# A long convolution with a gate: the first transform split by even and odd rows, in plain float32, with regrouped inputs

## The chip, the cores and the metric

The kernel runs on one core of a Trainium2 chip. The metric is the device time of one execution in microseconds (us). Matrix products run on TensorE (PE; its weight loads are PEld), elementwise work on VectorE (DVE), ScalarE (ACT) and GpSimd (POOL); SyncE (SP) and ACT issue the DMA transfers. The granted clock is the share of full speed that TensorE's clock was given.

## The reference

Four sequences of 12800 positions and 128 channels are convolved with a filter that a small network makes from `pos_emb`, multiplied by x, and sent through a gated projection. Cut to what matters:

```
h = maximum(pos_emb @ w1, 0) @ w2 * exp(-0.01 * pos)      # the filter
u = x * v                                                 # (4, 12800, 128) float32
y = x * irfft(rfft(u, 2 S) * rfft(h, 2 S))[:S]            # long convolution, S = 12800
gate = sigmoid(sum over k of conv_w[k] * y shifted by k)  # five taps
out = (gate * (y @ w_val)) @ w_out
```

Everything is float32, except that the weights of the gate arrive as 64-bit floats and are narrowed in the kernel.

## The kernel before

A position is written as s = 6400 j + 64 n1 + n2 with J = 2 blocks j, N1 = 100 and N2 = 64, and the Fourier transform of 6400 points is done in two steps, over n1 (a matrix of 100 by 100) and over n2 (one matrix of 64 by 64, complex, for each k1). The program has three phases.

The **first phase** (lines 179 to 307) does the step over n1. The signal part, `signal()` (lines 263 to 291), goes through 64 chunks, one for each j and each pair of n2 (P1C = 2). `fetch` (243 to 249) brings x and v of a chunk into one tile `ld`, 100 partitions (n1), in rows of 1 KB (two n2 by 128 channels); `_Split` (93 to 101) issues each transfer as one of 96 partitions and one of 4, on SP. `prep` (251 to 259) makes the product on DVE (`u_t`), a rounded copy on ACT (`u_hi`, of a type that TensorE reads in fewer steps than plain float32) and the remainder on POOL (`u_lo`). For two batches b at a time and for the cosine and the sine table (c), three matmuls of 512 columns are summed in one PSUM tile `fp`: hi x hi, table remainder x hi, hi x remainder (line 281). ACT empties the cosine tiles into `st` (284), DVE the sine tiles (286). Two stores per chunk then write `st` to `a_u` in DRAM (288 to 291), the cosine part from ACT's queue, the sine part from SP's.

Between the chunks runs the filter part, `filt()` (lines 184 to 237), in three sections: `pos_emb` is loaded with n1 in the partitions, transposed by TensorE (`tp`, 194), copied by DVE (`posT`, 198), multiplied by w1 (`gp`, 202) and cut and windowed by DVE into `g_sb` (206); then `ap` is the filter's step over n1, in plain float32 with two matmuls for the two halves of the output partitions (220, 221), copied by ACT to `ag` (222); last, for each k1, a scaled table `fk` is made by ACT and DVE (231, 232), multiplied (`gp`, 234) and copied back by ACT (236). The loop at lines 296 to 303 deals out the filter's steps among the 128 steps of the signal by a table of costs (297); a scheduler then sets the order on each engine by its own timing. PSUM has eight banks: four for `fp`, one for `tp`, one for `gp`, two for `ap`.

The **second phase** (313 to 430) reads `a_u` back for two k1 at a time, does the step over n2, multiplies by the filter's spectrum and goes back, in an order written out by hand, and writes `c_y`. The **third phase** (440 to 610) undoes the step over n1, transposes, and applies the gate.

## Time and profile before

| what | value |
|---|---|
| median of 3 runs | 1340.4 us (1333.96 to 1342.48) |
| the profiled execution | 1342.08 us, its span 1340.2 us |
| mean granted clock | 0.938 |
| PE / DVE / ACT / POOL busy | 88% / 80% / 47% / 52% of the span |
| moved by DMA | 332.90 MB, 248 GB/s over the span |
| first phase, to its last evacuation | 401 us, 109.55 MB moved |

The profile is of one execution. In its lists of groups a row is one line of the program on one engine: line, engine, operation, tile written <- tiles read, shapes, count | busy time in us, mean ns of one | idle time of the engine just before them and what ended it. A plain float32 matmul appears as two records, so a count of 128 there is 64 matmuls. In views by stretch of time a row gives the stretch, its length, then for each engine its busy time and, in brackets, the number of records, then the granted clock, the mean busy share of the 16 DMA engines and GB/s. In the order of time a row is start, length, engine, line, operation; where several records are merged, the length is that of all. In the DMA view, q1 holds what SP issues and q10 what ACT issues: packets, MB, share of the 16 engines' time in the stretch.

### The profile page before, as it was taken

Reading aid. Unit: us, or ns where it says so; the run is one execution under the profiler, and the core shown is the slowest. Engines: PE = TensorE matmul, PEld = TensorE weight load, DVE = VectorE, ACT = ScalarE, POOL = GpSimd, SP = SyncE. Lnnn points to the kernel's source line nnn. Section 1 sums busy time; section 2 is a strip of 40 time slices with the busy share of each in tenths; the row PEclk is TensorE's granted clock in tenths of the full one; section 3 lists DMA queues with packets and bytes.
Section 4 is the critical chain, followed back from the end, with each engine's and each line's share of the span. In section 5 each row is a group of like instructions: output and inputs, shape, how many; then the busy total and the mean of one; then the engine's idle time right before and its main releaser. Section 6 shows DMA issues by size and latency. Waiting matters only on the chain. (4 is left out here: it accounts for less than half of the span.)

```text
span 1340.2 us, 16163 instructions
## 1 busy us (share of the span) xinstructions
PE 1184.8 (88%) x5464; PEld 554.0 (41%) x5464; DVE 1068.8 (80%) x1130; ACT 635.5 (47%) x1064; POOL 693.8 (52%) x346
## 2 busy tenths in 40 slices
PE   4879999788686899999999999578999898999986
PEld 3657877566452333333333333122333333333332
DVE  5875343988456999999999999127999999999997
ACT  3334545677442333333333333134665666666663
POOL 2333234444454799999999999234333333333230
PEclk8888899889888999999999999656999999999999
DMA  9999788889987677778787874766989898889842
GB/s 250 285 312 297 232 253 271 245 268 306 296 261 285 219 278 280 281 277 279 280 280 279 280 266 173 209 160 157 254 236 246 234 243 243 244 247 243 241 145 98
DMA packets 144571, 332.90 MB, mean 248 GB/s; under 512 B 11166, under 2 KB 63434, under 8 KB 136554
## 3 DMA queue, kind: packets, MB, share of 16 engines
q1 hardware_dynamic: 96576, 226.13, 57.9%
q10 hardware_dynamic: 47914, 105.76, 21.7%
q8 instruction: 43, 0.70, 0.2%
q14 instruction: 38, 0.31, 0.1%
HBM read 200.77 MB, written 131.07 MB: 248 GB/s over the span
## 5 line engine op out<-in xcount | busy, mean ns | idle before, releaser
L534 DVE SCALAR_TENSOR_TENSOR gt<-ext,cw,gt 128x1600 f32<-128x1600 f32 x128 | 298.3, 2330 | 0.0
L258 POOL TENSOR_TENSOR u_lo<-u_t,u_hi 100x1024 fp32r<-100x1024 f32 x64 | 158.7, 2483 | 239.0 <-ACT u_hi L257 199.9
L519 POOL TENSOR_TENSOR ext<-yr,ld 128x400 f32<-128x400 f32 x120 | 134.1, 1117 | 280.4 <-DVE yr L517 275.1
L375 ACT COPY c_sb<-c_ps 128x1024 f32<-128x1024 f32 x100 | 101.3, 1013 | 275.3 <-PE c_ps L368 275.3
L340 PE MATMUL z_ps<-ld 128*64 128x512 f32 x800 | 194.4, 605 | 7.8 <-DMA ld<-a_u 6.6
L427 POOL TENSOR_TENSOR va<-va,vb 128x1024 f32<-128x1024 f32 x50 | 158.0, 3160 | 37.1 <-DVE vb L345 37.0
L281 PE MATMUL fp<-u_hi,fwd_hi 100*100 100x512 f32 x256 | 117.8, 460 | 55.2 <-ACT st L284 26.4
L492 PE MATMUL sd<-ld,inv 100*64 100x512 f32 x512 | 155.6, 681 | 9.8 <-issue 7.7
L286 DVE COPY st<-fp 100x512 f32<-100x512 f32 x128 | 85.4, 685 | 71.8 <-PE fp L281 52.9
L345 DVE TENSOR_TENSOR vb<-z_ps,h_sb 128x2048 f32<-128x2048 f32 x50 | 114.5, 2291 | 24.9 <-ACT c_sb L375 24.7
L506 PE MATMUL tp<-ident,sd_sb 128*128 128x128 f32 x512 | 90.7, 304 | 45.7 <-ACT sd_sb L499 45.7
L499 ACT COPY sd_sb<-sd 128x512 f32<-128x512 f32 x128 | 74.6, 583 | 115.5 <-PE sd L492 115.4
L553 PE MATMUL o_ps<-gd,wout 128*128 128x400 f32 x256 | 119.4, 548 | 8.4 <-DVE gd L548 8.2
L428 POOL TENSOR_TENSOR vc<-vc,vd 128x1024 f32<-128x1024 f32 x50 | 118.5, 2370 | 15.2 <-DVE vd L345 10.3
L256 DVE TENSOR_TENSOR u_t<-ld 100x1024 f32<-100x1024 f32 x64 | 86.9, 1359 | 48.4 <-POOL u_lo L258 33.6
L345 DVE TENSOR_TENSOR va<-z_ps,h_sb 128x2048 f32<-128x2048 f32 x50 | 114.0, 2281 | 11.0 <-DMA ld<-a_u 11.0
L429 POOL TENSOR_TENSOR va<-va,vb 128x1024 f32<-128x1024 f32 x50 | 118.6, 2371 | 0.0
L506 PEld LDWEIGHTS tp<-ident,sd_sb 128*128 128x128 f32 x512 | 58.6, 151 | 132.9 <-ACT sd_sb L499 132.9
L281 PE MATMUL fp<-u_hi,fwd_lo 100*100 100x512 f32 x256 | 110.0, 430 | 0.0
L368 PE MATMUL c_ps<-vc,ld 64*128 64x512 f32 x400 | 100.6, 621 | 10.7 <-DVE vc L418 10.6
L543 PE MATMUL v_ps<-ext,wval 128*128 128x400 f32 x256 | 108.5, 506 | 0.0
L257 ACT CAST u_hi<-u_t 100x1024 fp32r<-100x1024 f32 x64 | 68.0, 1064 | 77.4 <-PE fp L281 37.0
(76 smaller groups left out, 1895.6 us busy)
## 6 DMA issues: line engine op xcount, KB each, us to landing
c_y<-c_sb ACTq DMA_DIRECT2D x100, 512.0 KB
ld<-a_u SPq DMA_DIRECT2D x49, 1024.0 KB
ld<-c_y SPq DMA_DIRECT2D x64, 768.0 KB
ld<-in_xt_dram SPq DMA_DIRECT2D x32, 800.0 KB
out_dram<-o_sb ACTq DMA_DIRECT2D x32, 800.0 KB
ld<-in_x_dram SPq DMA_DIRECT2D x64, 384.0 KB
ld<-in_v_dram SPq DMA_DIRECT2D x64, 384.0 KB
a_u<-st ACTq DMA_DIRECT2D x64, 384.0 KB
```

The source lines that it names most:

```text
L258: nc.gpsimd.tensor_tensor(lo, u_t, hi.bitcast(F32), op=ALU.subtract)
L281: nc.tensor.matmul(out=fp, lhsT=w[:, c], rhs=d[:, b:b + 2], start=(k == 0), stop=(k == 2))
L340: nc.tensor.matmul(out=z[half[h]], lhsT=wk[:, h, half[c]], rhs=a2[:, h, j], start=True, stop=True)
L345: nc.vector.tensor_tensor(out, z.rearrange("p (b d) -> p b d", d=D).unsqueeze(1).to_broadcast([128, n, B, D]), h_sb.unsqueeze(2).to_broadc ...
L427: nc.gpsimd.tensor_tensor(va[:, 0:2], va[:, 0:2], vb[:, 0:2], op=ALU.add)
L428: nc.gpsimd.tensor_tensor(vc, vc, vd, op=ALU.add)
L429: nc.gpsimd.tensor_tensor(va[:, 2:4], va[:, 2:4], vb[:, 2:4], op=ALU.add)
L492: nc.tensor.matmul(out=sd[c * N2:(c + 1) * N2], lhsT=inv[:, c], rhs=ct[c][:, r * B * D:(r + 1) * B * D], start=True, stop=True)
L506: nc.tensor.transpose(out=tp[:, b], in_=t[:, b], identity=ident)
L519: nc.gpsimd.tensor_tensor(e[:, r0 + r], yr, xr, op=ALU.mult)
L534: nc.vector.scalar_tensor_tensor(gt, rows(t, k), cw[:, k:k + 1], gt, op0=ALU.mult, op1=ALU.add)
L553: nc.tensor.matmul(out=o_ps, lhsT=wout, rhs=gd, start=True, stop=True)
```

## The change

It has three parts, all in the first phase.

*Even and odd n1.* With n1 = 2 a + h, the transform's matrix at k1 + 50 equals that at k1 for even n1 and is its negative for odd n1. The 50 even rows are put into partitions 0 to 49 and the 50 odd ones into partitions 64 to 113, each with a table of 50 by 100 (50 k1, cosine and sine; `fwd2`). For each n2 of a chunk there are then two matmuls, `ev` and `od`, in two different row tiles of the array, 512 columns (4 batches by 128 channels), in plain float32, without the split into a rounded part and a remainder. ACT copies `od` to SBUF (`od_sb`); DVE writes `ev` + `od_sb` (k1 from 0 to 49) and `ev` - `od_sb` (k1 from 50 to 99) into `st`. The product is made on POOL for the even rows and on DVE for the odd ones, both on 50 partitions of 1024 columns. The PSUM banks are two each for `ev`, `od`, `gp` and `ap`. The stores of a chunk now hold the sums (ACT's queue) and the differences (SP's queue).

*x and v* are arranged by the host as one array `xv` in which a chunk's row of one partition (x and v, two n2, four batches) is contiguous, 8 KB; they are loaded three chunks ahead instead of two, the two halves of the partitions in separate transfers, each split into 48 and 2 partitions.

*Positions* are arranged as `post`, with (n2, feature) already in the partitions: the transposes `tp` and copies `posT` go, and one transfer of 128 partitions replaces four.

The core of the diff:

```diff
@@ -97,7 +102,8 @@
     def dma_start(self, out, in_):
-        for a, b in ((0, 96), (96, N1)):
+        n = out.shape[0]
+        for a, b in ((0, n // 16 * 16), (n // 16 * 16, n)):
             self.eng.dma_start(out=out[a:b], in_=in_[a:b])
...
+                pos_sb = load()[:, 0:J * HC // 2 * N1].rearrange("p (j q a) -> p j q a", j=J, q=HC // 2)
+                nc.sync.dma_start(out=pos_sb, in_=post[:, c0 // HC])
                 for j in range(J):
                     for n in range(0, HC, 8):
-                        tp = ps1.tile([128, 4, N1], F32, name="tp", bufs=1)
-                        for q in range(4):
-                            nc.tensor.transpose(
...
-                        nc.vector.tensor_copy(out=posT, in_=tp)
-                        yield
-                        gp = ps1.tile([N1, 8, FO], F32, name="gp", bufs=1)
+                        gp = ps1.tile([N1, 8, FO], F32, name="gp", bufs=2)
...
-                                lhsT=posT[:, q], rhs=w1bd, start=True, stop=True)
+                                lhsT=pos_sb[:, j, n // 2 + q], rhs=w1bd, start=True, stop=True)
...
+        H1 = N1 // 2
+        par = [slice(h * 64, h * 64 + H1) for h in range(2)]
...
             j, n0 = chunks[i]
...
+            t = load()
+            for h in range(2):
+                sync_s.dma_start(out=t[par[h]], in_=xv[j, h, n0 // P1C])
+            return t.rearrange("a (w e) -> a w e", w=2)
 
         def prep(i):
...
-            nc.vector.tensor_tensor(u_t, x_t, v_t, op=ALU.mult)
-            nc.scalar.copy(out=hi, in_=u_t)
-            nc.gpsimd.tensor_tensor(lo, u_t, hi.bitcast(F32), op=ALU.subtract)
-            return hi, lo
...
+            u_t = p1.tile([128, P1C, B * D], F32, name="u_t", bufs=3)
+            for h, eng in enumerate((nc.gpsimd, nc.vector)):
+                eng.tensor_tensor(
+                    u_t[par[h]].rearrange("a n e -> a (n e)"), t[par[h], 0], t[par[h], 1], op=ALU.mult)
+            return u_t
+
+        ahead = [fetch(0), fetch(1), fetch(2)]
...
-                for b in range(0, B, 2):
-                    for c in range(2):
-                        fp = ps1.tile([N1, 2, P1C, D], F32, name="fp", bufs=4)
-                        for k, (w, d) in enumerate(((fwd_hi, hi), (fwd_lo, hi), (fwd_hi, lo))):
-                            nc.tensor.matmul(out=fp, lhsT=w[:, c], rhs=d[:, b:b + 2], start=(k == 0), stop=(k == 2))
-                        o = st[:, c, :, b:b + 2].rearrange("k n b d -> k b n d")
-                        if c == 0:
-                            nc.scalar.copy(out=o, in_=fp)
-                        else:
-                            nc.vector.tensor_copy(out=o, in_=fp)
+                u_t = ready.pop(0)
+                st = p1.tile([N1, 2, P1C, B * D], F32, name="st", bufs=3)
+                for n in range(P1C):
+                    ev = ps1.tile([N1, B * D], F32, name="ev", bufs=2)
+                    od = ps1.tile([N1, B * D], F32, name="od", bufs=2)
+                    for h, o in enumerate((ev, od)):
+                        nc.tensor.matmul(out=o, lhsT=fwd2[par[h]], rhs=u_t[par[h], n], start=True, stop=True)
+                    od_sb = p1.tile([N1, B * D], F32, name="od_sb", bufs=2)
+                    nc.scalar.copy(out=od_sb, in_=od)
+                    nc.vector.tensor_tensor(st[:, 0, n], ev, od_sb, op=ALU.add)
+                    nc.vector.tensor_tensor(st[:, 1, n], ev, od_sb, op=ALU.subtract)
                     yield
-                for c in range(2):
-                    (scalar_s if c == 0 else sync_s).dma_start(
...
+                for s in range(2):
+                    (scalar_s if s == 0 else sync_s).dma_start(
+                        out=a_u[s * H1:(s + 1) * H1, :, ns, j].rearrange("k c n b d -> (k c) n (b d)"),
+                        in_=st[:, s])
```

The scheduler orders the new instructions anew. Two places matter below. The first is PE while the filter's `ap` matmuls run beside the signal's (the second section of `filt`). Before, the signal's matmuls come in runs between runs of the filter's:

```order
L220 MATMUL ap<-fwd,g_sb 64x100
L221 MATMUL ap<-fwd,g_sb 64x100
L281 MATMUL fp<-u_hi,fwd_hi 100x512
L281 MATMUL fp<-u_hi,fwd_lo 100x512
L281 MATMUL fp<-u_lo,fwd_hi 100x512
L281 MATMUL fp<-u_hi,fwd_hi 100x512
L281 MATMUL fp<-u_hi,fwd_lo 100x512
L281 MATMUL fp<-u_lo,fwd_hi 100x512
```

In the changed program (L208 and L209 are the filter's matmuls of before's L220 and L221, L267 is the signal's; `fwd_66` is the table `fwd2`):

```order
L208 MATMUL ap<-fwd,g_sb 64x100
L267 MATMUL ev<-u_t,fwd_66 100x512
L209 MATMUL ap<-fwd,g_sb 64x100
L267 MATMUL od<-u_t,fwd_66 100x512
L208 MATMUL ap<-fwd,g_sb 64x100
L209 MATMUL ap<-fwd,g_sb 64x100
```

The runs are cut up: an `ev` and its `od` are apart, with a filter matmul between them, and the shape changes from row tiles to column tiles and back around each.

The second place is DVE while the scalings `fk` run (the third section of `filt`). Before, two copies of `st` and one product stand between them for each chunk:

```order
L232 SCALAR_TENSOR_TENSOR fk<-dft,tw,fk 128x128
L286 COPY st<-fp 100x2x2x128 x2
L232 SCALAR_TENSOR_TENSOR fk<-dft,tw,fk 128x128 x4
L256 TENSOR_TENSOR u_t<-ld 100x1024
L232 SCALAR_TENSOR_TENSOR fk<-dft,tw,fk 128x128 x4
L286 COPY st<-fp 100x2x2x128 x2
```

In the changed program (L220 is now the scaling, L243 the product of the odd rows, L270 and L271 the sum and the difference):

```order
L243 TENSOR_TENSOR u_t<-ld 50x1024
L220 SCALAR_TENSOR_TENSOR fk<-dft,tw,fk 128x128 x4
L270 TENSOR_TENSOR st<-ev,od_sb 100x512
L271 TENSOR_TENSOR st<-ev,od_sb 100x512
L220 SCALAR_TENSOR_TENSOR fk<-dft,tw,fk 128x128 x4
L270 TENSOR_TENSOR st<-ev,od_sb 100x512
L271 TENSOR_TENSOR st<-ev,od_sb 100x512
L243 TENSOR_TENSOR u_t<-ld 50x1024
```

For each chunk four operations of 512 columns stand now where two stood; the scalings and the product keep their places.

63 lines of the change are left out of this document (21 added, 42 removed).

## The prediction

> **What bounds the kernel now.** I read the page first, then the busy time of the engines by stage, then the instructions of single lines by stage, and last the order of time inside the stage that matters.
>
> ```profile
> span 1340.2 us, 16163 instructions
> PE 1184.8 (88%) x5464; PEld 554.0 (41%) x5464; DVE 1068.8 (80%) x1130; ACT 635.5 (47%) x1064; POOL 693.8 (52%) x346
> ```
>
> These shares are means over three phases with different limits. The diff touches the first phase alone, so that phase has to be cut out. Its last store into `st` ends near 401 us. I cut it at the times at which 12, 36 and 52 of its 64 chunks were done:
>
> ```profile
> 0.00:94.00 94.00, 63.91 (x294) 46.56 (x295) 63.58 (x113) 30.21 (x46) 32.38 (x17) 0.87 0.96 281
> 94.00:253.00 159.00, 152.56 (x1137) 116.56 (x1136) 76.22 (x93) 82.38 (x121) 58.10 (x24) 0.95 0.88 263
> 253.00:346.00 93.00, 74.52 (x358) 55.36 (x356) 76.43 (x130) 66.72 (x149) 41.60 (x18) 0.91 0.90 279
> 346.00:401.00 55.00, 42.25 (x144) 26.45 (x144) 28.46 (x34) 23.02 (x36) 26.82 (x11) 0.84 0.87 280
> 401.00:1340.20 939.20, 851.60 (x3536) 309.04 (x3536) 824.09 (x764) 433.21 (x714) 534.89 (x278) 0.95 0.75 238
> ```
>
> The columns are length, PE, PEld, DVE, ACT and POOL busy, then granted clock, DMA share and GB/s. Stage 1 (0 to 94) belongs to the DMA engines: share 0.96, no engine over 64 of 94 us. Stage 2 (94 to 253) belongs to PE, busy 152.56 of 159. Stage 3 (253 to 346) belongs to nobody alone: DVE 76.43 and PE 74.52 of 93, DMA 0.90. Stage 4 is transfers again (0.87), with every engine below 43 of 55. How many chunks a stage holds is read from the evacuations on DVE, two per chunk, and what else DVE does in stage 3 from line 232:
>
> ```profile
> 0.00:94.00 94.00, 15.97 (x24) 0.87 0.96 281
> 94.00:253.00 159.00, 32.30 (x48) 0.95 0.88 263
> 253.00:346.00 93.00, 21.08 (x33) 0.91 0.90 279
> 346.00:401.00 55.00, 15.95 (x25) 0.84 0.87 280
> ...
> 253.00:346.00 93.00, 38.60 (x80) 0.91 0.90 279
> ```
>
> So stage 2 is where the filter's transform (L220, L221) runs between the signal's matmuls, and stage 3 is where 80 of the 100 `fk` scalings (38.60 us of DVE) run between the signal's evacuations. The 939 us behind 401 have the same instructions in both kernels and are taken as unchanged.
>
> **The change part by part.** Prices first.
>
> ```profile
> L281 PE MATMUL fp<-u_hi,fwd_hi 100*100 100x512 f32 x256 | 117.8, 460 | 55.2 <-ACT st L284 26.4 <-ACT u_hi L257 18.5 <-DVE st L286 9.6
> L256 DVE TENSOR_TENSOR u_t<-ld 100x1024 f32<-100x1024 f32 x64 | 86.9, 1359 | 48.4 <-POOL u_lo L258 33.6 <-DMA a_u<-st 9.5 <-DMA ld<-in_x_dram 3.1
> L286 DVE COPY st<-fp 100x512 f32<-100x512 f32 x128 | 85.4, 685 | 71.8 <-PE fp L281 52.9 <-DMA a_u<-st 18.8
> L232 DVE SCALAR_TENSOR_TENSOR fk<-dft,tw,fk 128x128 f32<-128x128 f32 x100 | 48.9, 538 | 10.3 <-ACT fk L231 10.3
> L234 PE MATMUL gp<-fk,ag 128*128 128x128 f32 x200 | 29.2, 291 | 4.4 <-ACT ag L236 3.2 <-DVE fk L232 1.2
> L202 PE MATMUL gp<-w1bd,posT 128*100 128x128 f32 x128 | 19.8, 305 | 2.8 <-DVE posT L198 2.8
> ...
> L548 DVE TENSOR_TENSOR gd<-v_ps,sg 128x400 f32<-128x400 f32 x128 | 71.6, 559 | 3.5 <-PE v_ps L543 2.3 <-ACT sg L538 1.1
> L516 DVE TENSOR_TENSOR yr<-tp,dif 128x204 f32<-128x204 f32 x128 | 46.0, 360 | 63.6 <-ACT dif L508 44.7 <-DMA ld<-c_y 18.7 <-ACT o_sb L561 0.2
> ```
>
> DVE. Two copies of 512 columns per chunk (L286) become four sums and differences of one PSUM and one SBUF operand. That form is at L548 (400 columns, 559 ns) and L516 (204 columns, 360 ns): 199 ns for 196 columns, so 512 columns take 559 + 114 = 673 ns, about what the copy takes. Net: two more per chunk, 1.35 us per chunk, 86 us over the phase. The product (L256) stays, since 50 partitions of 1024 columns take as long as 100; half of it goes to POOL, in the place of `u_lo`. The 16 copies of `posT` leave DVE. ACT loses the cast (L257) and keeps one evacuation of 512 columns per column n, into `od_sb` now. A wait is added there: ACT's store of a chunk waited for ACT's own copies and now waits for DVE's second sum, and the next `od_sb` copies, which DVE's next sums need, stand behind it.
>
> ```profile
> 181.58 0.72 ACTq L101 DMA_DIRECT2D a_u<-st  x2
> ...
> L284 ACT COPY st<-fp 100x512 f32<-100x512 f32 x128 | 70.9, 592 | 70.2 <-PE fp L281 46.4 <-DMA a_u<-st 15.6 <-DMA ld<-in_v_dram 5.6
> ```
>
> From there ACT needs 0.72 + 0.59 = 1.3 us, while DVE still has a difference and a product to do, 0.67 + 1.36 = 2.0 us: covered. Uncovered, 1.3 - 0.7 = 0.6 us a chunk would be 10 us in the 16 chunks of stage 3, within the upper end below.
>
> PE. Three matmuls of 512 columns for each of four PSUM tiles become one `ev` and one `od` in plain float32 for each of two columns n. In order of time, first the seam of stage 2, then a plain float32 row-tile pair of the second phase, and the weight loads beside the latter:
>
> ```profile
> 180.14 0.31 PE L221 MATMUL ap<-fwd,g_sb 100*64 100x100 f32 x1
> 180.38 0.47 PE L281 MATMUL fp<-u_hi,fwd_hi 100*100 100x512 f32 x1
> ...
> 182.50 0.31 PE L221 MATMUL ap<-fwd,g_sb 100*64 100x100 f32 x1
> ...
> 182.65 0.31 PE L221 MATMUL ap<-fwd,g_sb 100*64 100x100 f32 x1
> ...
> 184.13 0.39 PE L281 MATMUL fp<-u_hi,fwd_lo 100*100 100x512 f32 x1
> 184.36 0.40 PE L281 MATMUL fp<-u_lo,fwd_hi 100*100 100x512 f32 x1
> 184.69 0.39 PE L220 MATMUL ap<-fwd,g_sb 100*64 100x100 f32 x1
> ...
> 521.98 1.99 PE L368 MATMUL c_ps<-va,ld 64*128 64x512 f32 x8
> 523.90 1.08 PE L327 MATMUL z_ps<-w2bd,ag 128*64 128x256 f32 x8
> ...
> 522.52 0.19 PEld L368 LDWEIGHTS c_ps<-va,ld 64*128 64x128 f32 x2 [0.24 <-issue]
> 522.95 0.19 PEld L368 LDWEIGHTS c_ps<-va,ld 64*128 64x128 f32 x2 [0.24 <-issue]
> ```
>
> At full clock an old matmul takes 0.23 us (184.13 to 184.36). A plain float32 matmul has two records; in the second phase each takes a step of 0.43 us (522.52 to 522.95) whether one or both halves of the rows work in it, so a pair takes 0.86 us and a lone one also 0.86. Eight records, two pairs, take 1.92 us (521.98 to 523.90). A filter matmul pair takes two steps of 0.15 (182.50 to 182.65). A change of shape costs 0.10 more than the same step without it (184.36 to 184.69 is 0.33; 180.14 to 180.38 is 0.24).
>
> In the order of the changed program, the `ev` and `od` of stages 1 and 4 mostly stand side by side (18 and 23 pairs), and PE has room there. In stage 2 the scheduler puts filter matmuls between them. Counted from its rows for chunks 12 to 36: 4 pairs and 88 lone ones, 147 pairs and 55 lone filter matmuls, 178 changes of shape. Before, the same chunks have 288 old matmuls, 185 pairs and 14 lone filter matmuls, 78 changes of shape, and 56 small matmuls (transposes, L202, L234) against 11 now, 0.3 us each by L202 and L234. After: 92 x 0.86 + 202 x 0.29 + 178 x 0.10 + 3 = 159 us. Before: 288 x 0.233 + 199 x 0.29 + 78 x 0.10 + 17 = 150 us. Stage 2 took 159 us, 9 us more than its sum. Below, if PE never waits: 159, no change; above, if the small matmuls are priced at full clock (17 becomes 12) and the remainder stays: +13. I take **+10**.
>
> DVE in stage 3: 76.43 + 32 x 0.673 = 98 us, and 84 instead of 80 scalings, 2 more: 100 us in a stage of 93. Below, without any idle time: +7; above, with all of the 16.6 us in which DVE now idles there: +24. DVE will seldom wait in a stage that it limits, so about 3 us of idle: **+10**.
>
> Transfers. Bytes stay; x and v come in rows of 8 KB instead of 1 KB, in the same number of issues on SP (four loads of 48 and 2 partitions per chunk for four of 96 and 4), and with three chunks ahead instead of two. Queue q1 in stages 1 and 4, in the second phase (4 and 8 KB rows to 128 partitions) and in the third (8 KB rows to 96), and q10 (2 KB stores) in stage 2:
>
> ```profile
> q1 hardware_dynamic: 16895, 20.98, 76.4%
> ...
> q1 hardware_dynamic: 6945, 10.18, 57.7%
> ...
> q1 hardware_dynamic: 13351, 56.68, 41.6%
> ...
> q1 hardware_dynamic: 11868, 75.90, 63.1%
> ...
> q10 hardware_dynamic: 5060, 9.42, 19.4%
> ```
>
> The second column is MB, the third the share of 16 engines. Bytes per engine and ns: 18.3 now (20.98 MB in 0.764 x 94 us x 16), 21.3 in the second phase (0.416 x 400 us x 16), 15.7 in the third (0.631 x 480 us x 16). Stage 1 loads some 16 MB (20.98 less the stores), 55 us of all engines; at 21.3 it gains 8 us, at 15.7 it loses 9. Stage 4 loads 5 MB: 3 us either way. The new loads reach fewer partitions at once than either row; between ends that far apart I take **0** for both stages and keep the ends. DVE there needs 63.6 + 24 x 0.67 less 7 for `posT`, 73 of 94 us, and 45 of 55: hidden under the transfers.
>
> Sum: 0 + 10 + 10 + 0 = +20 on a span of 1340.2, so 1360. The profiled execution is within 2 us of the median of the runs, 1340.4, so the same 20 gives **1360 us**.
>
> [...]
>
> **The rivals.**
>
> *Lone row tiles overlap after all* (faster): PE starts `od` while `ev` still runs, with the filter's short matmuls slipped through. For it: pairs do overlap in the second phase. Against: every change of shape in the rows above costs time, and the filter's weights fill 100 rows, both tiles. Price: 88 lone matmuls become 44 pairs, 38 us less on PE; stage 2 then falls to its transfers, 0.88 of 159 or 140 us, some 20 us shorter, and with -8, +7 and -3 elsewhere: 1316.
>
> *Gains and losses cancel* (no change): loads run at 21.3 in stages 1 and 4 (-8, -3) and PE does not wait in stage 2 (0), since the chain product, cast, remainder is gone, while DVE still costs 10: 1339.
>
> *Loads to half of the partitions run at half the rate* (slower), 10.7: 4.8 us of loads per chunk and 2.7 us of stores (q10: 9.42 MB in 0.194 x 159 us x 16, 19.1), 7.5 us x 64 = 480 against 401: 1419. For it: the third phase's 15.7 on 96 partitions against 21.3 on 128. Against: loads and stores of different engines interleave.
>
> *DVE is shut out by POOL* (slower). The products read two SBUF operands on both engines at once now:
>
> ```profile
> L256 DVE TENSOR_TENSOR u_t<-ld x64: 1207/1217/3405, 7.1 to 392.3; 100x1024 f32<-100x1024 f32 x64
> ```
>
> Its longest is 2.19 us over its median, about one POOL operation. If that met every chunk of stage 3, 16 x 2.19 = 35 us come on top of the forecast's 20: 1395. Against: the mean, 1359 ns, says that it met few of 64 so far, and POOL ran as often.
>
> That the transform isn't done as row tiles is no rival for the end: side by side they save PE time only where PE has room.
>
> **How the numbers follow.** Chances: forecast 0.46, own range from -8 - 0 + 7 - 3 to +9 + 13 + 24 + 3, 1336 to 1389; lone tiles overlap 0.13; cancel 0.22; half rate 0.09; shut out 0.10. What a measurement of this kernel can tell from no change is about 1%, 13 us. Faster takes nearly all of the first rival and a little of the second: 0.16. Slower takes three quarters of the forecast, 0.35, and both slow rivals, 0.19, in all 0.54. Within 1% is left with 0.30. The range leaves out most of the first rival and of the half rate: 1322 to 1400.
>
> **What would show it.** Cut at 12, 36 and 52 chunks again, stage 2 should be 160 to 172 us with PE above 0.95 and nearly all `ev` and `od` lone; stage 3 100 to 110 us with DVE above 0.93; the sum or difference near 0.67 us; stage 1 and 4 within 9 and 3 us of 94 and 55. The forecast is wrong if PE idles in stage 2 or if stage 3 ends by a transfer, if q1 runs below 15 bytes per engine and ns (half rate), or if the product on DVE has a mean above 2 us (shut out).

## The result, and the profile after

The changed kernel takes **1521.2 us** (median of 4 runs, 1513.15 to 1526.54) where the kernel before takes 1341.4 on the same chip: a ratio of 1.136, 95% interval 1.129 to 1.142. The forecast was 1360 in a range of 1322 to 1400: the sign is right and the size far off. A few executions of a kernel are over 1.5% longer than its fastest; the ratios here and below leave these out, so they differ a little from the quotient of the medians. The page of the profiled execution begins:

```profile
span 1521.4 us, 15786 instructions
...
PE 1377.4 (91%) x5144; PEld 533.2 (35%) x5144; DVE 1160.1 (76%) x1240; ACT 578.1 (38%) x1000; POOL 689.4 (45%) x346
...
PEclk9775555555566557999999999995599999999999
```

PE has 193 us more of busy time than before, with fewer records of matmuls (5144 against 5464). The line of the granted clock says where: from the fourth slice on, for most of the first phase, TensorE had half its clock. The first phase is cut again at the times at which 12, 36, 52 and 64 chunks were done, in the columns of the prediction:

```profile
0.00:126.50 126.50, 85.32 (x305) 43.70 (x306) 75.12 (x127) 20.54 (x38) 35.44 (x19) 0.81 0.94 230
126.50:398.00 271.50, 268.56 (x914) 107.50 (x912) 117.05 (x129) 57.33 (x90) 57.84 (x25) 0.51 0.62 147
398.00:526.20 128.20, 123.89 (x302) 55.83 (x302) 100.23 (x164) 53.71 (x136) 39.88 (x16) 0.58 0.80 201
526.20:583.40 57.20, 45.95 (x92) 17.44 (x88) 45.75 (x59) 13.09 (x23) 21.07 (x9) 0.50 0.86 258
583.40:1521.40 938.00, 853.65 (x3536) 308.71 (x3536) 821.90 (x763) 433.40 (x714) 535.21 (x278) 0.95 0.77 238
```

Behind the first phase nothing has changed (938.0 us, 939.2 before). Stage 2 has grown from 159 to 271.5 us, stage 1 from 94 to 126.5, stage 3 from 93 to 128.2. In stage 2 PE is busy for 0.99 of the time, as it was for 0.96 before, but at a clock of 0.51 where it had 0.95. In order of time its middle reads:

```profile
236.52 2.03 PE L267 MATMUL ev<-u_t,fwd 50*100 50x512 f32 x2
238.48 0.43 PE L209 MATMUL ap<-fwd,g_sb 100*64 100x100 f32 x1
238.49 0.43 PE L208 MATMUL ap<-fwd,g_sb 100*64 100x100 f32 x1
238.70 0.37 PE L209 MATMUL ap<-fwd,g_sb 100*64 100x100 f32 x1
238.71 0.37 PE L208 MATMUL ap<-fwd,g_sb 100*64 100x100 f32 x1
239.01 2.02 PE L267 MATMUL od<-u_t,fwd 50*100 50x512 f32 x2
```

From 236.52 to 238.48, 1.96 us for a lone `ev`, which was priced at 0.86 without the changes of shape. The order is the forecast one, `ev` and `od` apart with filter matmuls between them; the price is not. Three more rows of the page bear on stages 1 and 3:

```profile
L243 POOL TENSOR_TENSOR u_t<-ld 50x1024 f32<-50x1024 f32 x64 | 154.0, 2407 | 417.8 <-PE ev L267 292.5
...
L270 DVE TENSOR_TENSOR st<-ev,od_sb 100x512 f32<-100x512 f32 x128 | 88.2, 689 | 204.0 <-PE ev L267 109.3
...
L243 DVE TENSOR_TENSOR u_t<-ld 50x1024 f32<-50x1024 f32 x64 | 115.0, 1796 | 22.6 <-DMA ld<-in_xv_dram 20.8
```

The sum of `ev` and `od_sb` takes 0.69 us, near the 0.67 that was worked out. But DVE's product, on half the partitions, has a mean of 1796 ns where the whole product had 1359: it runs beside POOL's, which reads SBUF too (part 6 takes POOL's away).

### The profile page after: what moved, and what is told of

It reads as the page before. It is cut to its first block, busy times and chain, and to the rows that moved or that the text cites. A ratio compares the mean times of both kernels' runs of the same rounds, so it can differ in the third digit from the quotient of the medians.

```text
span 1521.4 us, 15786 instructions
## 1 busy us (share of the span) xinstructions
PE 1377.4 (91%) x5144; PEld 533.2 (35%) x5144; DVE 1160.1 (76%) x1240; ACT 578.1 (38%) x1000; POOL 689.4 (45%) x346
## 4 chain that ended last, share of the span: by engine, by line
PE 32%; DVE 22%; issue 3%; ACT 2%; DMA 1%; POOL 1%; SPq 0%; ACTq 0%; DVEq 0%; POOLq 0%
DVE gt L519 14%; PE c_ps L353 12%; PE z_ps L325 11%; DVE gd L533 3%; PE z_ps L312 3%; PE sd L477 3%; DVE yr L501 2%; DVE yr L502 2%; PE tp L491 2%; ACT sd_sb L484 1%; PE v_ps L528 1%; DVE vc L403 1%; PE o_ps L538 1%; POOL vc L413 0%; POOL va L414 0%
## 5 line engine op out<-in xcount | busy, mean ns | idle before, releaser
L243 POOL TENSOR_TENSOR u_t<-ld 50x1024 f32<-50x1024 f32 x64 | 154.0, 2407 | 417.8 <-PE ev L267 292.5
L267 PE MATMUL od<-u_t,fwd 50*100 50x512 f32 x256 | 233.3, 1030 | 33.6 <-ACT od_sb L269 33.6
L270 DVE TENSOR_TENSOR st<-ev,od_sb 100x512 f32<-100x512 f32 x128 | 88.2, 689 | 204.0 <-PE ev L267 109.3
L267 PE MATMUL ev<-u_t,fwd 50*100 50x512 f32 x256 | 230.8, 1019 | 13.9 <-POOL u_t L243 8.3
L269 ACT COPY od_sb<-od 100x512 f32<-100x512 f32 x128 | 74.8, 594 | 288.4 <-PE od L267 125.0
L243 DVE TENSOR_TENSOR u_t<-ld 50x1024 f32<-50x1024 f32 x64 | 115.0, 1796 | 22.6 <-DMA ld<-in_xv_dram 20.8
```

Source lines behind the costliest of these rows:

```text
L243: eng.tensor_tensor(u_t[par[h]].rearrange("a n e -> a (n e)"), t[par[h], 0], t[par[h], 1], op=ALU.mult)
L267: nc.tensor.matmul(out=o, lhsT=fwd2[par[h]], rhs=u_t[par[h], n], start=True, stop=True)
```

## The experiments

Each ratio is against runs of the kernel before on the same chip (medians of 1341.8 to 1348.1 us). Two theories stood at the start. A: the clock is down because matmuls of 50 lone rows leave most of the array without work. B: it is down for another reason, and other rows change nothing.

### 1. Full rows: is it the clock, and is it the rows?

```diff
-    fwd2 = np.zeros((128, N1))
-    fwd2[:N1 // 2], fwd2[64:64 + N1 // 2] = half[:, 0], half[:, 1]
+    fwd2 = np.zeros((128, 2, N1))
+    fwd2[:N1 // 2, 0], fwd2[64:64 + N1 // 2, 1] = half[:, 0], half[:, 1]
...
-  nc.tensor.matmul(out=o, lhsT=fwd2[par[h]], rhs=u_t[par[h], n], start=True, stop=True)
+  nc.tensor.matmul(out=o, lhsT=fwd2[0:64 + H1, h], rhs=u_t[0:64 + H1, n], start=True, stop=True)
```

(Not shown: the rows of `u_t` between the halves are zeroed once.)

> The changed kernel with one thing different: each signal matmul works on partitions 0 to 113 in one piece, with a table that is zero on the other half's rows (and the gap rows of u_t zeroed once), instead of on 50 partitions in a row tile. Count, length, results and evacuations stay. Theory A (TensorE's granted clock falls to half because a lone row tile keeps too little of the array at work): the clock in chunks 12 to 36 returns to above 0.9 and that stage falls from 271 us to about 165 to 185, the whole to about 1420. Rival B (the clock falls because of the many changes of shape or because of plain float32 as such): clock stays near 0.5, stage stays near 270, the whole within 15 us of 1521.

Measured: **1400.9 us**, ratio 1.046 (1.040 to 1.053). Its stages:

```profile
0.00:129.20 129.20, 86.57 (x355) 48.09 (x356) 73.49 (x120) 23.35 (x42) 38.97 (x19) 0.85 0.92 230
129.20:299.30 170.10, 167.64 (x883) 87.39 (x882) 121.41 (x149) 57.12 (x99) 57.52 (x25) 0.99 0.92 230
299.30:401.60 102.30, 83.32 (x282) 39.33 (x281) 95.79 (x155) 49.54 (x124) 38.82 (x17) 0.97 0.91 244
```

The same number of matmuls, none of them in a row tile: the clock is back (0.99 where it was 0.51), stage 2 takes 170.1 and stage 3 102.3 us. So 120 us of the 180 hang on the rows, by way of the clock. These two stages are those of the prediction (160 to 172, 100 to 110), which had priced all of PE at full clock. Stage 1 does not move.

### 2. Pairs in PE's order

Every matmul of the first phase keeps the order of the program, so that `ev` and `od` stand side by side:

```diff
-  nc.tensor.matmul(out=o, lhsT=fwd2[par[h]], rhs=u_t[par[h], n], start=True, stop=True)
+  tc.keep_in_program_order(
+      nc.tensor.matmul(out=o, lhsT=fwd2[par[h]], rhs=u_t[par[h], n], start=True, stop=True))
```

(and the same around the filter's.)

> The changed kernel with PE's order in the first phase pinned to program order, so that every ev stands next to its od (128 pairs instead of 71 or fewer, 146 seams between signal and filter instead of some 235). Theory A: two row tiles at work at once count as 100 rows, the clock in chunks 12 to 36 rises to 0.9 and the stage falls below 160 us, the whole to about 1410. If the lone tiles cost only their length and the clock follows something else: PE's work halves there but at half clock, the stage takes about 180 to 200 us and the clock stays near 0.5, the whole about 1440.

Measured: **1410.7 us**, ratio 1.053 (1.046 to 1.061). The number is theory A's, the reason is not:

```profile
130.10:289.10 159.00, 148.89 (x822) 72.94 (x818) 109.86 (x120) 49.37 (x75) 68.96 (x24) 0.52 0.91 255
```

Stage 2 takes 159 us *at half clock*. Two row tiles side by side took the time of one: in order of time a pair takes 1.97 us here (215.94 to 217.91), as long as the lone `ev` above (1.96). That makes up for the clock but did not bring it back (0.52). A right total would have hidden this; the clock column showed it. Theory A, that any full use of the rows raises the clock, was in doubt from here.

### 3. The clock by itself

Four kernels do nothing but plain float32 matmuls from fixed tiles, in stretches, each behind matmuls of 128 rows that bring the clock to 1.0. (In the second of them the mean clock of the whole run was 0.934, which its one stretch at 0.50, 50 rounds of 2.48 us by the row below, an estimated 124 of 938 us, makes by itself.) In the last, 20 rounds of a lone row tile and a column pair then bring it to 0.5: the mean of that run was 0.724, where the stretches seen at 0.50 alone, 268 us of 903, would have left 0.85. The form of the first:

```diff
+        for f, k in ((rows114, 70), (lone, 70), (pair, 45), (rows72, 70), (rows100, 70), (col, 120), (mixed, 35), (mixed114, 35)):
+            full(40)
+            for i in range(k):
+                f(i)
```

> Computes none of the reference: only plain float32 matmuls from fixed SBUF tiles, in stretches, each behind 40 matmuls of 128 rows that should bring the clock to 1.0. Stretches: 70 of 114 rows x 100 columns; 70 lone ones of 50 rows (one row tile); 45 pairs of 50 rows in both row tiles; 70 of 72 rows; 70 of 100 rows; 120 pairs of column tiles of 100 rows with 100 moving columns; 35 rounds of lone row tile, column pair, lone row tile, column pair; the same with 114 rows in the place of the row tiles. Theory A, the clock follows the share of the array that works: 0.5 in the lone row tiles, and in 72 rows less than in 114, but 1.0 in the 45 pairs (0.86 us a pair, some 39 us). Theory C, matmuls in row tiles do not hold the clock up however they are paired, which the clock of 0.52 in stage 2 of the kernel with pinned pairs speaks for: 0.5 in lone and paired row tiles (1.7 us a pair, 76 us), 1.0 with 72, 100 and 114 rows. Theory D, the changes of shape in the mixture pull the clock down: 1.0 in all plain stretches, 0.5 in the mixtures only.

In rows by stretch of time (length, PE, PEld, ACT, POOL, clock, DMA, GB/s), lone row tiles, column pairs, the mixture with row tiles, the mixture with 114 rows:

```profile
135.00:195.00 60.00, 60.00 (x141) 22.74 (x140) 0.00 (x0) 0.00 (x0) 1.00 0.00 0
...
492.00:512.00 20.00, 20.00 (x472) 20.00 (x469) 0.00 (x0) 0.00 (x0) 1.00 0.02 3
555.00:717.00 162.00, 162.00 (x391) 45.43 (x390) 0.00 (x0) 0.00 (x0) 0.50 0.00 0
760.00:848.00 88.00, 88.00 (x391) 29.12 (x390) 0.00 (x0) 0.00 (x0) 1.00 0.00 1
```

Lone row tiles ran at full clock: 1.00 over 60 us, 141 records of 0.43 us each. Theories A and C both fall. Only the mixture with row tiles was slow (0.50 over 162 us), not every mixture as theory D had it (1.00 over 88 us with 114 rows). PE is busy without a gap in all four.

> Computes none of the reference: plain float32 matmuls from fixed SBUF tiles again, in stretches behind 60 matmuls of 128 rows each. A row tile is a lone matmul of 50 rows and 512 columns, a column pair two of 100 rows into two column tiles with 100 moving columns. Stretches: 40 rounds of row tile and whole matmul; 50 of row tile and one column pair; 30 of row tile and eight column pairs; 12 of four row tiles and eight column pairs; 40 of a pair of row tiles and one column pair; 16 of a pair of row tiles and sixteen column pairs; 50 of whole matmul and one column pair. If any change out of row tiles pulls the clock down: 0.5 in the first. If it takes the change between row tiles and column tiles: 1.0 in the first and in the last, 0.5 in the second and the fifth. If it is the number of changes per time, 1.0 comes back in the stretches with eight or sixteen column pairs or four row tiles to a round; if it is the mixture as such, they stay at 0.5.

```profile
198.00:313.00 115.00, 115.00 (x278) 32.18 (x276) 0.00 (x0) 0.00 (x0) 0.50 0.00 0
368.00:444.00 76.00, 76.00 (x1011) 48.94 (x1012) 0.00 (x0) 0.00 (x0) 1.00 0.01 2
...
831.00:899.00 68.00, 68.00 (x300) 24.55 (x299) 0.00 (x0) 0.00 (x0) 1.00 0.00 0
```

Of seven mixtures only the first shown, a lone row tile and one column pair in turn, is at 0.5. With eight column pairs (second row), with a whole matmul in the place of the row tile (third), with four row tiles to eight pairs (60 us), with a pair of row tiles to one column pair or to sixteen (53 and 62 us), or with a whole matmul in the place of the column pair (83 us): 1.00. So it is no change of shape as such.

What orders all of this is an estimate of the author's, worked out from these stretches, the **work of the array per time**: the share of the 128 rows that a matmul uses, times the time in which its columns stream at full clock (0.86 us for 512, 0.17 for a column pair: 20 us for 472 records), over the time that the round takes. Back-to-back lone tiles: 50/128 = 0.39. Row tile and column pair: a round with a whole matmul in its place takes 68 us x 6/300 = 1.36 us at full clock, and by that the work is (0.39 x 0.86 + 0.78 x 0.17)/1.36 = 0.34. The next kernel was made to look for a threshold of this estimate:

> Computes none of the reference: plain float32 matmuls from fixed tiles in nine stretches, each behind 60 matmuls of 128 rows: 50 rows x 50 columns of the array, 512 moving columns; 100 rows x 64 columns; 32 rows x 100 columns; whole matmuls with 128, 64 and 32 moving columns; lone row tiles of 50 rows with 256, 128 and 64 moving columns. If the clock follows the share of the array's rows at work: 0.5 with 32 rows (a quarter), 1.0 with 50 x 50 and 100 x 64, and 0.5 in lone row tiles as soon as short matmuls leave gaps between them. If it follows the share of all cells: 0.5 with 50 x 50 too. If the clock only asks for an unbroken run of matmuls: 1.0 in all three long forms and 0.5 only where short matmuls leave gaps, for whole ones as for row tiles.

50 rows by 50 columns of the array; 32 rows; whole matmuls of 64 and of 32 columns; lone row tiles of 128 and of 64 columns:

```profile
59.00:118.00 59.00, 59.00 (x139) 16.78 (x138) 0.00 (x0) 0.00 (x0) 1.00 0.00 0
...
288.00:397.00 109.00, 109.00 (x129) 36.39 (x128) 0.00 (x0) 0.00 (x0) 0.50 0.00 0
...
560.00:626.00 66.00, 66.00 (x594) 66.00 (x593) 0.00 (x0) 0.00 (x0) 1.00 0.00 1
683.00:801.00 118.00, 118.00 (x555) 118.00 (x554) 0.00 (x0) 0.00 (x0) 0.50 0.00 1
...
968.00:1022.00 54.00, 54.00 (x496) 53.86 (x494) 0.00 (x0) 0.00 (x0) 1.00 0.01 1
1079.00:1169.00 90.00, 90.00 (x543) 90.00 (x542) 0.00 (x0) 0.00 (x0) 0.50 0.00 1
```

32 rows back to back, 0.25 by the estimate, lost the clock (0.50 over 109 us) though PE was never idle; so it isn't an unbroken run that counted. Whole matmuls of 64 columns, 0.107 of every 0.222 us, 0.48, kept it; of 32 columns, 0.24, lost it. Lone tiles of 128 columns, 0.39 x 0.215/0.218 = 0.38, kept it; of 64 columns, 0.19, lost it. Fewer columns of the array did not cost it: 50 x 50 (first row) and 100 x 64 stayed at 1.00 over 59 us each. The expectation's threshold of one half is too high: the stretches that kept the clock reach down to 0.38, those that lost it up to 0.34.

> Computes none of the reference: plain float32 matmuls from fixed tiles in five stretches; ahead of each, 60 matmuls of 128 rows and then 20 rounds of lone row tile and one column pair, which bring the clock to 0.5. Then: 50 lone row tiles; 40 pairs of row tiles; 50 matmuls of 72 rows; 40 rounds of a pair and one column pair; 40 rounds of a whole matmul and one column pair. If the clock follows the work that the array does per unit of time, counted in full-speed work, a lone row tile at half clock does only a quarter and stays at 0.5 for its whole stretch (1.7 us each, 85 us), where it ran at 1.0 when it started from there; pairs and 72 rows do one half and come back to 1.0 within some us (0.86 us each). The mixtures do 0.42 to 0.45 at half clock, as they leave gaps: undecided, but both alike. If the clock follows the share of time in which rows are at work, whatever the clock, lone row tiles come back to 1.0 as the others do.

Started from half clock: lone row tiles, pairs, 72 rows, a pair with a column pair, a whole matmul with a column pair:

```profile
103.00:188.00 85.00, 85.00 (x100) 28.38 (x99) 0.00 (x0) 0.00 (x0) 0.50 0.00 0
292.00:323.00 31.00, 31.00 (x148) 12.07 (x146) 0.00 (x0) 0.00 (x0) 1.00 0.00 1
422.00:507.00 85.00, 85.00 (x101) 28.89 (x100) 0.00 (x0) 0.00 (x0) 0.50 0.00 0
607.00:705.00 98.00, 98.00 (x316) 27.54 (x312) 0.00 (x0) 0.00 (x0) 0.50 0.00 1
814.00:863.00 49.00, 49.00 (x216) 17.71 (x216) 0.00 (x0) 0.00 (x0) 1.00 0.00 0
```

The lone tiles that held full clock in the first of these kernels did not come back to it from half: 85 us at 0.50. By the estimate they do half the work per time there, 0.195. Pairs (100 of 128 rows, 0.39 at half clock) came back (1.00); 72 rows (0.28) did not (0.50 over 85 us), against the expectation, which had counted them as a whole array; the rows in use order the two. A pair with a column pair, 0.78 x (0.86 + 0.17) in 98 us x 8/316 = 2.48 us, 0.32, stayed at 0.50; a whole matmul with a column pair, (0.86 + 0.78 x 0.17) in such a round, 0.40, came back, so the two mixtures were not alike. One threshold between 0.34 and 0.38, estimated from these stretches and counted in full-speed work, fits every one of them, those from full and those from half. Lone row tiles stayed where they started, at 1.00 for 60 us and at 0.50 for 85.

By the prediction's own counts, stage 2 of the changed kernel does (4 x 0.39 x 0.86 + 8.4 x 0.78 x 0.17)/6.6 = 0.37 per chunk at full clock, on the edge, and 2.45/11.3 = 0.22 once the clock is down: by the estimate it does not return. With full rows, (4 x 0.89 x 0.86 + 1.11)/7.1 = 0.59. Before, 12 matmuls of 0.23: (12 x 0.78 x 0.23 + 1.11)/6.6 = 0.49.

The trace of the changed kernel shows when the clock was lost. All through stage 1 it goes up and down (0.63 to 0.93 in slices of 10 us from 50 to 110), and then PE does this:

```profile
106.02 1.10 PE L267 MATMUL od<-u_t,fwd 50*100 50x512 f32 x2 [1.14 <-ACT od_sb L269]
...
108.33 1.84 PE L267 MATMUL ev<-u_t,fwd 50*100 50x512 f32 x2
```

The `ev` already takes 1.84 us. In the 3.8 us ahead of it, from 104.56 on, PE waited 1.14 us for ACT and did one `od` and 16 records of column tiles, four pairs: (0.39 x 0.86 + 4 x 0.78 x 0.17)/3.8 = 0.23. From 110 to 380 us every slice of 10 us is at 0.50. The kernel before has such dips too, 0.74 from 100 to 110 us and 0.78 from 130 to 140, and is back at 1.00 two slices later. So what stage 2 of the changed kernel shows is a clock that stayed at 0.50 for 270 us once it was there. That its mixture, at 0.37, would pull down a full clock by itself is argued from the count and not shown.

### 4. The threshold in the kernel itself

First a try that came before the threshold was estimated: the filter's column tiles out of the mixture (it leaves out the sine part of the filter; the core of its diff).

```diff
-  nc.tensor.matmul(out=ap[0:N2, e], lhsT=lhs, rhs=fwd[:, wr], **fl)
-  nc.tensor.matmul(out=ap[N2:2 * N2, e], lhsT=lhs, rhs=fwd[:, wi], **fl)
+  nc.tensor.matmul(out=ap[:, e], lhsT=lhs, rhs=fwd[:, wr], **fl)
```

> The changed kernel with the filter's two matmuls into two column tiles replaced by one matmul of 128 columns, which leaves the sine part of the filter out and puts other columns in its place; the signal's row tiles stay as they are and stay lone. If row tiles among column tiles are what halves the clock, stage 2 runs at 0.9 or more and takes 155 to 175 us in the place of 271.5, stage 3 some 20 us less than 128, and the whole 1390 to 1425. If any change out of row tiles does it, the clock stays near 0.5 in stage 2 and the time near 1521.

Measured: 1469.0 us, ratio 1.092 (1.083 to 1.100). Stage 2 takes 241.1 us at a clock of 0.54: without column tiles the clock is as low. Then work that nobody needs:

```diff
+  nc.tensor.matmul(out=ev, lhsT=fwd2[0:64 + H1], rhs=u_t[0:64 + H1, n], start=True, stop=True)
   for h, o in enumerate((ev, od)):
       nc.tensor.matmul(out=o, lhsT=fwd2[par[h]], rhs=u_t[par[h], n], start=True, stop=True)
```

> The changed kernel with one more matmul of 114 rows ahead of each ev, into the same PSUM tile, which the ev then overwrites: two needless matmuls of 0.86 us at full clock in each chunk. Lone row tiles and column tiles stay as they are. If the clock follows the share of the array that works, it comes back to 0.9 or more in stage 2: 6.6 us a chunk by the prediction's sum plus 1.72 and two more changes of shape, some 8.7 us a chunk or 210 us in the place of 271.5, and the whole 1430 to 1460, faster for having more to do. If mixing row tiles with other shapes is what costs the clock, PE stays at 0.5 and the added 3.4 us a chunk make stage 2 350 us and the whole 1600.

Measured: **1508.8 us**, ratio 1.124 (1.118 to 1.131). Neither the 1430 to 1460 nor the 1600. All of stage 2, and then two stretches in it:

```profile
137.70:380.40 242.70, 242.70 (x947) 97.04 (x948) 91.20 (x121) 48.16 (x73) 56.62 (x25) 0.71 0.68 165
```

```profile
157.00:262.00 105.00, 105.00 (x316) 36.52 (x314) 31.61 (x41) 18.18 (x28) 18.90 (x8) 0.50 0.57 131
293.00:361.00 68.00, 68.00 (x348) 31.70 (x346) 32.98 (x44) 15.84 (x25) 21.29 (x9) 1.00 0.84 206
```

Two matmuls of 114 rows more per chunk, and stage 2 is 29 us *shorter* than in the changed kernel (the whole is some 12 us shorter, by ratios whose intervals just touch: 1.118 to 1.131 against 1.129 to 1.142). It lives in both states: 105 us at half clock (3.0 records a us), then 68 at full (5.1). A chunk has 947/24 = 39.5 records, 7.7 us at full clock and 13 at half. Its work is 2.45 + 2 x 0.89 x 0.86 = 3.98, so 0.52 at full clock, over the estimated threshold, and 0.31 at half, under it: by the estimate it would stay in either state until something else moved it. What moved it was not followed up. But lone row tiles stand among column tiles at 1.00 for 68 us here, so it is not the mixture as such that costs the clock.

### 5. The loads

```diff
-            for h in range(2):
-                sync_s.dma_start(out=t[par[h]], in_=xv[j, h, n0 // P1C])
+            nc.sync.dma_start(out=t, in_=xv[j, n0 // P1C])
```

with `xv` filled up to 128 rows by zeros.

> The changed kernel with x and v padded with zero rows, so that a chunk is one transfer to all 128 partitions (28% more bytes) instead of two to halves, each split. Theory C (a load to half of the partitions at a time runs at a low rate, which made chunks 0 to 12 take 126 us instead of 94): q1 moves over 18 bytes per engine and ns there instead of some 15, and these chunks take 95 to 110 us; chunks 12 to 36 stay near 270 at half clock; the whole about 1500. Rival (loads don't matter, the first chunks are slow because of the clock too): the first chunks stay above 120 us, the whole within 10 us of 1521.

Measured: 1486.7 us (the middle of two runs, 1475.1 and 1498.4). Its first stage takes 100.0 us where the changed kernel's takes 126.5, and q1 moves 23.2 bytes per engine and ns there (28.76 MB in 0.774 x 100 us x 16) where it moved 15.1 (23.61 MB in 0.773 x 126.5 us x 16). The loads by themselves:

> Computes none of the reference: only the loads of x and v, in six stretches of 24 chunks of 0.82 MB with no stores beside them: rows of 1 KB to 96 and 4 partitions (as before), 8 KB rows to two halves one behind the other (as in the change), 8 KB rows to 96 and 4 partitions, 8 KB rows to 128 partitions with zeros (1.05 MB), the two halves from two queues at once, and both halves into partitions 0 to 49. If loads to half of the partitions are what costs stage 1 its 33 us, the halves one behind the other take clearly longer per chunk than 1 KB rows to 96 and 4 partitions (3.6 us or more against 2.8 by the 18.3 bytes per engine and ns of stage 1), as slow as both halves into partitions 0 to 49, and the two queues at once are faster. Rival: the size of the rows does it: all 8 KB forms to fewer than 128 partitions take the same time. Rival: it is only the meeting with the stores: all forms take the same time here, 2.3 to 2.8 us a chunk.

1 KB rows to 96 and 4 partitions, halves, 8 KB rows to 96 and 4, padded to 128, and both halves into partitions 0 to 49 (length, POOL, clock, DMA share, GB/s):

```profile
20.00:84.00 64.00, 0.00 (x0) 1.00 0.91 235
100.00:190.00 90.00, 0.00 (x0) 1.00 0.75 169
215.00:280.00 65.00, 0.00 (x0) 1.00 0.94 232
300.00:345.00 45.00, 0.00 (x0) 1.00 1.02 414
...
520.00:640.00 120.00, 0.00 (x0) 1.00 0.64 115
```

By themselves, then, 8 KB rows were no faster than 1 KB rows (232 and 235 GB/s). Halves ran at 169 GB/s: a chunk of 0.82 MB takes 4.85 us in the place of 3.5, and from two queues at once they were no faster (164 GB/s in that stretch). They were faster than loads that go to one half alone (115), so the second half added something. To 128 partitions it was 414, or 323 without the zeros.

What the two other parts do alone, on the kernel before with its split transform: both layouts with x and v to 96 and 4 partitions,

> The kernel before with only the layouts of the change: x and v in rows of 8 KB on 100 partitions (split 96 and 4), positions already transposed; the transform stays in three matmuls of the rounded kind. If the layouts by themselves are harmless (theory A: it is the transform that costs): 1315 to 1345, with the clock in chunks 12 to 36 above 0.9. Rival (8 KB rows are slow whatever the transform): first 12 chunks above 110 us, the whole above 1360.

1337.7 us, ratio 0.993 (0.988 to 0.998), but with another share of the stages: stage 1 takes 114.1 us in the place of 94, as the rival said of that stage, and stage 2 146.1 in the place of 159. And the positions alone,

> The kernel before with one of the three parts: positions laid out in blocks, without transposes and their copies; x and v are loaded as before and the split transform stays. If the contiguous blocks of x and v cost stage 1 some 20 us (114 against 94 in the kernel with both layouts) and the positions alone bring stage 2 from 159 to 146, this is 13 to 20 us under before: 1322 to 1330. Rival: what stage 2 gains is given back in stages 3 and 4, which transfers limit: 1337 to 1342.

1349.4 us, ratio 1.000 (0.996 to 1.004): a miss. Stage 2 was 151.8 us in the place of 159, but stage 1 took 102.2 in the place of 94. Its queue q1 moved 23.98 MB in stage 1 where it had moved 20.98, as the loads run further ahead there (21 chunks issued in the place of 17); 3.0 MB at the 288 GB/s of that stage are an estimated 10 us, more than the 8 that it grew by. The further 12 us of both layouts together (114.1 against 102.2, at 265 GB/s against 288, one profiled execution each) come with the new layout of x and v, though its loads cost nothing by themselves (232 against 235); why is open.

### 6. POOL beside DVE, and what is left

Full rows and whole loads together (the matmuls over 114 rows):

> The matmuls over 114 rows with zeros and the loads to 128 partitions in one kernel. If clock and loads are two separate costs, stage 1 ends near 100 us (129 with full rows alone), stage 2 stays near 170, stage 3 near 102: 1365 to 1375. If full rows already gave back what the loads cost, 1400.

1381.4 us, ratio 1.027 (1.019 to 1.034); stage 1 is back from 129 to 106 us: the two costs add up. Then the product of a chunk by DVE alone, in one operation (the matmuls now use all 128 rows, since no row of `u_t` is left unwritten):

```diff
-            for h, eng in enumerate((nc.gpsimd, nc.vector)):
-                eng.tensor_tensor(
-                    u_t[par[h]].rearrange("a n e -> a (n e)"), t[par[h], 0], t[par[h], 1], op=ALU.mult)
+            nc.vector.tensor_tensor(u_t.rearrange("a n e -> a (n e)"), t[:, 0], t[:, 1], op=ALU.mult)
```

> Full rows and whole loads again, with the product of a chunk made by DVE alone in one operation on 128 partitions, and none on POOL. If POOL shuts DVE out of its second operand, the product falls from 1.8 us to 1.2 to 1.3, stage 3 from 104 us to 95 to 99, and the whole from 1381 to 1365 to 1376. If the operations were long for another reason, or stage 3 is held by something else, 1378 to 1385.

Measured: **1338.4 us**, ratio 0.9985 (0.994 to 1.003), 43 us less by the medians and 38 by the ratios, where 5 to 16 were expected. DVE in stage 3 with POOL's product beside it:

```profile
L220 DVE SCALAR_TENSOR_TENSOR fk<-dft,tw,fk 128x128 f32<-128x128 f32 x72 | 39.9, 615 | 0.4
...
L246 DVE TENSOR_TENSOR u_t<-ld 50x1024 f32<-50x1024 f32 x16 | 21.0, 1312 | 0.9 <-PE ev L270 0.5
```

and without it:

```profile
L243 DVE TENSOR_TENSOR u_t<-ld 128x1024 f32<-128x1024 f32 x17 | 20.7, 1217 | 2.3 <-PE ev L266 2.3
L220 DVE SCALAR_TENSOR_TENSOR fk<-dft,tw,fk 128x128 f32<-128x128 f32 x70 | 19.8, 345 | 0.0
```

The expectation looked at the product alone. The scalings `fk`, which read two SBUF operands too, were held up more: 615 ns against 345, 20 us of DVE where stage 3 fell by 22 (103.7 to 81.7). In stage 2 it was the product, 2105 ns against 1216. The sums, which read one operand from PSUM, did not change (679 and 680 ns in stage 2). Part of this cost is older than the change: in stage 3 of the kernel before, beside POOL's `u_lo`, the scalings took 532 ns.

With loads and product mended so, the three ways of placing the matmuls can be compared. Lone row tiles:

> The changed kernel with whole loads and the product on DVE alone in one operation; the matmuls stay lone row tiles. Against full rows with the same loads and product (1338) only the rows of the matmuls differ. If the clock is what is left of the cost: stage 2 at 0.5 and 235 to 255 us, the whole 1420 to 1450. If the product on POOL had a part in the clock (PE waiting for it): stage 2 under 200 us and the whole under 1390.

1425.1 us, ratio 1.064 (1.059 to 1.069), 87 us over full rows; stage 2 at 0.52 and 228.7 us. The clock fell here without loads to halves and without a product on POOL. Pairs in order:

> The changed kernel with whole loads, the product on DVE alone, and the row tiles kept side by side in PE's order. A pair takes at half clock what a full-row matmul takes at full clock, so PE needs per chunk of stage 2 no more than 2 x 1.7 us and the filter's share: 5.2 us, 125 us in all, and the stage goes to its transfers, 130 to 150 us against 165 with full rows; stage 1 at 96, stage 3 at 80: 1305 to 1325, faster than before. Rival: the order written out makes PE, ACT and DVE wait for each other as in the first kernel with pinned pairs (stage 2 159, stage 3 115): 1345 to 1370.

1338.2 us, ratio 0.996 (0.992 to 0.999): a miss. Stage 2 did go to 149.5 us, but stages 1, 3 and 4 together lost 21 against full rows. That is the rival's kind of loss, but not its time (1345 to 1370). (A pair at half clock took 1.97 us in part 2; a matmul of 114 rows at full clock took 0.85 in part 3, 60 us for 141 records, so a pair stands beside two of these, not one.) Plain float32 without row tiles or joins, cosine and sine apart:

> The kernel with the positions alone in blocks, and the transform in plain float32 over all 100 rows, cosine and sine tables apart, without the split into rounded part and remainder and without row tiles and joins. By 0.86 us for a plain float32 matmul against three times 0.23, PE needs 0.64 us a chunk more: stage 2 goes from 152 to 167 us and the whole from 1336.5 (its span with the split) to 1350; clock above 0.9. Rival: the chain of product, cast and remainder that goes was what PE waited for in the other stages, and the whole stays at 1336 or falls under it.

1351.7 us, ratio 1.003 (0.998 to 1.008): plain float32 by itself is not what costs. In the profiled execution (span 1364.9 us) stage 2 takes 163.1 us with PE busy all of it at a clock of 1.00. Last, pairs in order for chunks 12 to 39 and full rows elsewhere (the core of its diff; the filter's column tiles are kept in order as well):

```diff
+                        r = par[h] if i in PAIRED else slice(0, 128)
+                        mm = nc.tensor.matmul(out=o, lhsT=fwd2[r, h], rhs=u_t[r, n], start=True, stop=True)
+                        if i in PAIRED:
+                            tc.keep_in_program_order(mm)
```

> Full rows, whole loads and the product on DVE, but for chunks 12 to 39 the row tiles, kept side by side in PE's order with the filter's column tiles between them. By the stages of the two kernels that it is made of (full rows 96, 165, 82, 53; pairs 104, 149.5, 91, 57.5), the better of each gives 96 + 149.5 + 82 + 53 + 938 = 1318: faster than before by 1.5 to 2%. Rival: stage 3 pays back what stage 2 gains, because the transfers (0.99 of stage 3 with full rows) are then later than the work: 1330 to 1340.

Measured: **1326.2 us**, ratio **0.987** (0.983 to 0.992): 1.3% less than the kernel before, between the 1318 that was expected and the rival's 1330 to 1340.

```profile
90.10:239.30 149.20, 139.05 (x832) 72.42 (x832) 89.39 (x122) 50.70 (x75) 0.00 (x0) 0.60 0.94 311
239.30:325.70 86.40, 84.30 (x370) 45.25 (x371) 73.24 (x145) 50.10 (x121) 0.00 (x0) 0.86 0.97 332
```

In stage 2 the transfers are now the busiest (0.94; PE 139 of 149), and it is 15 us shorter than with full rows although the clock is at 0.60. By the estimate above its work is at the edge: 48 pairs and 640 records of column tiles, 160 pairs, make (48 x 0.78 x 0.86 + 160 x 0.78 x 0.17)/149.2 = 0.36, and the clock goes up and down (0.50 to 0.94 in slices of 10 us).

## Why the prediction was wrong, step by step

Stage lengths in us; the last three columns undo one cost after the other:

| stage | before | forecast | after | full rows | + whole loads | + product on DVE |
|---|---|---|---|---|---|---|
| 1 | 94 | 94 | 126.5 | 129.2 | 106.3 | 96.4 |
| 2 | 159 | 169 | 271.5 | 170.1 | 172.7 | 164.7 |
| 3 | 93 | 103 | 128.2 | 102.3 | 103.7 | 81.7 |
| 4 | 55 | 55 | 57.2 | 63.0 | 56.7 | 52.8 |
| rest | 939 | 939 | 938.0 | 936.9 | 934.5 | 937.6 |
| median | 1341 | 1360 | 1521 | 1401 | 1381 | 1338 |

**The step that failed is "at full clock an old matmul takes 0.23 us" and what was built on it**: every price of PE was read from stretches at full clock (its stages have a mean of 0.95) and carried over to a stage whose matmuls use 50 of 128 rows. The sum of stage 2, 159 us, was right as a count and as an order, and kernels with full rows gave 165 to 173 where 169 was forecast. The clock was taken as a given of the stage, though the prediction quoted it in the rows by stage. Here it was an outcome of what PE was given to do (0.51 with lone row tiles, 0.99 with full rows): by the estimate of part 3 the change put 0.37 of work per time in the place of 0.49, and 0.22 once the clock was down, and it stayed at 0.50 up to 380 us. That cost 101 us in stage 2 and 26 in stage 3, which full rows give back (9 of it are lost again in stages 1 and 4).

The busy share of PE does not tell the clock: PE was busy for 0.99 of stage 2 at a clock of 0.51, and for 0.99 of that stage with full rows at 0.99; and it had no gap in the stretch of 32 rows at 0.50, nor in that of 50 rows at 1.00. All stretches of matmuls alone ran at 0.50 or at 1.00, and what told which was the estimate of part 3, the rows in use times the time in which columns stream, per time.

**Stage 1, "0 with both ends kept" (-8 to +9): mis-sized.** It became +32.5. The rival of loads at half rate had the right price, 4.8 us of loads a chunk of 0.82 MB; the loads alone took 4.85. That rate, 10.7 bytes per engine and ns, half of the second phase's 21.3, was the author's estimate and is shown by no run as such; in its place q1 moved 15.1 in stage 1, and loads to two halves alone moved 169 GB/s where those to 96 and 4 partitions moved 235. The rival's chance of 0.09 leaned on loads and stores of different engines interleaving, but beside its stores stage 1 moved 230 GB/s where it had moved 281. The rival was wrong about reach: past stage 1 the transfers are not what ends (0.62 of stage 2). The rate is not all of the 32.5 us. Stage 1 also moved more, 29.12 MB in the place of 26.40, as loads were issued for 20 chunks in the place of 17 before the twelfth was done: at 281 GB/s that would be 104 us, 10 more than before, and the lower rate makes it 126.5, some 23 more. The first of these two was in no term of the sum, though the prediction names the third chunk ahead. By themselves one transfer to 128 partitions ran at 414 GB/s, 96 and 4 partitions at 235 and 232, the two halves at 169 one behind the other and at 164 from two queues, and loads to 50 partitions of one half at 115.

**Stage 3, "+10 by DVE": right once the clock is back** (102.3 us, DVE 95.79 of it). But the price of DVE hid another: POOL's product held up the scalings (615 ns against 345) and the product (2105 against 1216 in stage 2). That was the rival "shut out", priced at 35 us on top; taking it away gave 38 by the ratios (41 between the two profiled spans: 22 in stage 3, 10 and 8 in stages 1 and 2, 4 in stage 4, less 3 behind), part of which the kernel before had been paying for `u_lo`. So both slow rivals were true, beside a third cost that had none.

**The signs that were named missed it.** The forecast was to be wrong if PE idled in stage 2 (it was busy for 0.99), if stage 3 ended by a transfer (PE was busy for 123.89 of its 128.2 us), if q1 ran below 15 bytes per engine and ns in stage 1 (15.1), or if the product on DVE had a mean above 2 us (1.80). None came about, with the time 161 us off: two of them named costs that were real, with limits that these did not reach, and none looked at the clock. Only the lengths of stages 1 to 3 and DVE's share of stage 3 (0.78 where more than 0.93 was named) showed that something was wrong.

**Right as forecast:** the order of `ev` and `od`, the sum at 0.69 us, stage 4 within 3 us, nothing behind the first phase, and *lone row tiles overlap after all* not coming true (no `od` starts within its `ev` in the rows shown of stage 2).

## What to carry to other kernels

When a change makes PE's matmuls narrower, work out the rows in use times the streaming time, per time, before and after. Here, in the stretches of matmuls alone, 0.34 and less by this estimate ran at a clock of 0.50 and 0.38 and more at 1.00 when started from full clock; started from 0.50, 0.39 and 0.40 brought 1.00 back and 0.32 did not. In the changed kernel, at 0.51, the prices read at full clock did not hold (1.96 us for a lone `ev` priced at 0.86). Read the clock column of a stage next to its busy share: stage 2 of the changed kernel, 0.99 busy at a clock of 0.51, did too little in its matmuls by this estimate (0.22), and wider matmuls with zeros (170.1 us at 0.99) or two tiles side by side (159 us at 0.52) both mended its time, by different means. Operations of DVE that read two SBUF operands got longer beside POOL's product (1216 to 2105 ns, 345 to 615), sums with one operand in PSUM did not: look at everything on DVE that shares the time, not only at the pair that was split.
